# Moving four output gates and the third ranking to later steps, and replacing the last accumulating scatter, in an mLSTM and mixture-of-depths kernel

## The chip, the cores and the metric

The kernel runs on one core of a Trainium2 chip. The metric is device time in microseconds (us) of one execution, the median of several. A profile records one execution: every instruction of the five engines with its start and its duration, and the DMA transfers. The engines are TensorE (PE in the profile; its weight loads are PEld), VectorE (DVE), ScalarE (ACT), GpSimd (POOL) and SyncE (SP). Each works through its own instructions in program order and waits on semaphores for the others. Here SP issues nearly all plain DMAs, and POOL issues the indirect ones (rows by a list of indices).

## What is computed

An mLSTM cell runs over 768 time steps for 4 batches of 8 heads of 40 channels. Its output is seen as x of shape (4, 768, 320). A mixture-of-depths layer then picks the 128 best of the 768 rows of each batch and adds a gated two-layer network to these rows only:

```python
# per step t: m_new = max(f + m, i); f_stab = exp(f + m - m_new); i_stab = exp(i - m_new)
C = f_stab * C + i_stab * outer(v, k)
n = f_stab * n + i_stab * k
y = sigmoid(o_gate) * (C @ q) / max(abs(n . q), 1)
...
scores = x @ w_gate                       # (4, 768)
top = the 128 largest scores of a batch
ye = relu(x[top] @ w1) @ w2               # 320 -> 1024 -> 320
out = x.copy()
out[top] = x[top] + sigmoid(scores[top])[:, None] * ye
```

All data are 32-bit floats.

## The kernel before

The 768 time steps of a batch are cut into three chunks of 256, so that the loop over n (line 590) has 12 steps; step n works on batch b = n // 3. Steps 0 to 2 are batch 0, steps 9 to 11 batch 3. The order of all instructions is written out by hand (`manual_schedule`): what a Python call emits first comes first on its engine.

A step has these parts, in this order:

- `load(n + 3)` (line 78) has SP issue the loads of step n + 3: v (two DMAs), k (two), q (one), and gate loads `load_o` (line 70; four DMAs for one step). Three buffers hold k, q and v, four hold the gates. The dictionaries in `load` also place some stores between the loads, and they decide which gates go with which load: in the kernel before, the gates of steps 6, 7 and 8 follow q of step 9, the gate of step 9 follows q of step 10, and those of steps 10 and 11 come when `load(12)` is called, in step 9.
- `scores(n)` and `masked(n)`: the products of k and q on PE, and the causal mask on DVE (line 313).
- `turn(n + 1, "kT")` (line 232): PE transposes k of the next step, ACT copies the result out of PSUM. Its `count` is a number of filler products (`fill`, line 227) on PE ahead of the transposes, given by a tuple for steps 0 to 7. `widen` (line 223) copies q on ACT, and `turn(n + 1, "qT")` does for q what the other does for k.
- `update` and `states` (lines 266 and 278): the products of k and the weighted v on PE, and the running states on DVE. `weigh(n)` (line 248) makes the weighted v, two POOL instructions.
- `read(n)` and `attend(n)` (lines 317 and 334): the two parts of the numerator, on PE; `divide(n)` (line 343): the division on DVE, which gives y.
- `sigmoid(n)` (line 256, ACT) turns the gate into its sigmoid, `output(n)` (line 356, POOL, two instructions) multiplies it with y and writes x, `store(n)` (line 364, SP, two DMAs) writes x to the output, and `router(n)` (line 371, DVE, two products with `wg`) makes the scores of the step's 256 rows.

Once the scores of a batch are complete, the rows are ranked. `spread` (line 399) has PE write the 768 scores of the batch to all partitions and ACT copy them (`sb`). `ranks` (line 421) counts, for every row, how many scores are greater: three of the six groups of 128 rows on DVE (`greater`, line 414), three on ACT (`signs`, line 419). `select` makes a 0/1 matrix of rows and ranks, `numbers` gets the row numbers from it with small products on PE and four DVE instructions (`index`, line 457), and `fetch` (line 501) is an indirect DMA on POOL that gathers the 128 picked rows from the output in HBM into `xe`. `fetched` transposes them, `layer1` and `layer2` are the network on PE, `valued` makes the gate g of the picked rows. `weighed` (line 561) scales the result by g on ACT, and `add` (line 566) is an indirect DMA on POOL that adds it onto the rows in HBM.

The first batch's network runs in step 8, the second's in steps 9 and 10, the third's in step 11 and after the loop. The fourth batch is handled after the loop without a gather: `picked` multiplies x with the 0/1 matrix on PE. The third batch's scores are spread at the end of step 9 and ranked in step 10, beside `layer2(1)`. Where gates 6 and 7 are concerned, their sigmoids and outputs stand at the end of step 8, those of step 8 in the middle of step 9.

Two sizes that matter here: `ps_t` has two PSUM buffers shared by the transposes, by `layer2`'s result and by `fetched`; `ps_s`, `ps_u` and `ps_h` have one each.

Of the kernel before, what the change touches and what calls it, by code (L numbers as in the profile page):

```python
# [9 lines left out]
FP = mybir.dt.float32  # L10
# [3 lines left out]
OP = mybir.AluOpType  # L14
# [12 lines left out]
def _fast(ctx, tc, q, k, v, i_gate, f_gate, o_gate, w_gate, w1_in, w2_in, out):  # L27
# [6 lines left out]
    NS = S // 256  # L34
# [43 lines left out]
    def load(n):  # L78

        if n < N:  # L80
            load_kv(n, v_t, v)
            load_kv(n, k_t, k)
            for i in {8: (2,), 9: (3, 4, 5)}.get(n, ()):
                store(i)
            load_q(n)
            for i in {7: (0, 1)}.get(n, ()):
                store(i)
        for i in {7: (), 8: (), 9: (6, 7, 8), 11: (), 12: (10, 11)}.get(n, (n - 1,) if n <= N else ()):
            load_o(i)

    for t, src in ((f_sb, f_gate), (i_sb, i_gate)):
# [164 lines left out]
    def sigmoid(n):  # L256
        ACT.activation(out=o_t[n % NO], in_=o_t[n % NO], func=AF.Sigmoid)  # L257
# [98 lines left out]
    def output(n):  # L356
        b, s = divmod(n, NS)
        for r in range(2):
            x, o = x_t[b % 2][:, 2 * s + r, 0:DM], o_t[n % NO][:, r].rearrange("s h d -> s (h d)")
            order = "s (p j d) -> s j p d"  # L360
            POOL.tensor_tensor(out=x.rearrange(order, j=2, d=D), in0=pending[n]["y"][:, r].rearrange("s (j p) d -> s j p d", j=2),  # L361
                               in1=o.rearrange(order, j=2, d=D), op=OP.mult)

    def store(n):
        b, s = divmod(n, NS)
        for c in range(2):
            a = 256 * s + 128 * c
            SP.dma_start(out=out[b, a:a + 128, :].rearrange("(r t) d -> t r d", t=64),  # L368
                          in_=x_t[b % 2][64 * c:64 * c + 64, 2 * s:2 * s + 2, 0:DM])

    def router(n):
        b, s = divmod(n, NS)
        x = x_t[b % 2][:, 2 * s:2 * s + 2]
        scr = work.tile([128, DM], FP, name="scr", bufs=1)
        for r in range(2):
            DVE.tensor_tensor_reduce(out=scr, in0=x[:, r, 0:DM], in1=wg, scale=1.0, scalar=0.0,  # L376
                                     op0=OP.mult, op1=OP.add, accum_out=x[:, r, DM:DM + 1])
        del pending[n]
# [17 lines left out]

    dep = {}

    def spread(b, r0, r1):

        x, w = x_t[b % 2], r1 - r0
        pB = ps_s.tile([128, 2, 512], FP, name="pB", tag="s")
        for r in range(w):
            PE.transpose(pB[:, r // 4, 128 * (r % 4):128 * (r % 4) + 128],
                         x[:, r0 + r, DM:DM + 1].to_broadcast([128, 128]), ident)
        flat = pB.rearrange("p j t -> p (j t)")[:, 0:128 * w]
        sb = mod.tile([128, 128 * w], FP, name=f"sb{w}", bufs=1)
        ACT.copy(out=sb, in_=flat)
        return sb
# [11 lines left out]
    def ranks(b):  # L421
        x, d = x_t[b % 2], dep[b]
        d["cnt"] = mod.tile([128, 2 * NS], FP, name="cnt")
        for r in range(2 * NS):
            (greater if r < NS else signs)(b, d["sb"], x[:, r, DM:DM + 1], d["cnt"][:, r:r + 1])
        DVE.tensor_scalar(out=d["cnt"][:, NS:], in0=d["cnt"][:, NS:], scalar1=-0.5, scalar2=0.5 * (S - 1),
                          op0=OP.mult, op1=OP.add)

    def ranks_first(b):

# [120 lines left out]
    def layer2(b, f0=0, f1=NF):  # L551
        d = dep[b]
        if f0 == 0:
            if b < B - 1:
                d["py"] = ps_t.tile([128, DM], FP, name="py", tag="t")
            else:
                d["py"] = ps_h.tile([128, 2, 512], FP, name="py", tag="h")[:, 0, 0:DM]
        for f in range(f0, f1):
            PE.matmul(d["py"], d["hT"][:, f, :], w2[:, f, :], start=(f == 0), stop=(f == NF - 1))  # L559

    def weighed(b):
        d = dep[b]
        d["yg"] = mod.tile([128, DM], FP, name="yg")
        ACT.activation(out=d["yg"], in_=d["py"], func=AF.Copy, scale=d["g"])  # L564

    def add(b):
        d = dep.pop(b)
        POOL.indirect_dma_start(out=out[0:b + 1].rearrange("b s d -> (b s) d"),  # L568
                                out_offset=bass.IndirectOffsetOnAxis(ap=d["idx"], axis=0),
                                in_=d["yg"], in_offset=None, bounds_check=(b + 1) * S - 1, oob_is_err=False,  # L570
                                compute_op=OP.add)

    causal()
    other(POOL, wv_t[0])
# [15 lines left out]
    for n in range(N):  # L590
        b, s = divmod(n, NS)
        more = n + 1 < N
        late = b > 1 and s == 1
        given = late or n == 5
        if n > 0:
            load(n + 3)
        if n == 5:
            for h in range(2):
                f, g = slice(512 * h, 512 * h + 512), slice(2 * h, 2 * h + 2)
                SP.dma_start(out=w1[:, :, f], in_=w1_in[0:256, f].rearrange("(j p) f -> p j f", j=2))  # L600
                for i in range(2):
                    SP.dma_start(out=w1c[64 * i:64 * i + 64, g],
                                 in_=w1_in[256:DM, :].rearrange("p (f i e) -> p i f e", i=2, e=128)[:, i, g])
            for h in range(2):
                SP.dma_start(out=w2[:, 4 * h:4 * h + 4], in_=w2_in[512 * h:512 * h + 512].rearrange("(f p) d -> p f d", p=128))
        for i in {10: (9,), 11: (10,)}.get(n, ()):
            store(i)
        scores(n)
        masked(n)
        if n == 8:  # L610
            fetched(0)
            numbers(1, ps_t.tile([128, 3], FP, name="pi", tag="t"))
            fetch(1)
        if n == 8:
            valued(0)
        if n == 0:
            update(0)
            load(3)
            states(0)
        if n == 8:  # L620
            layer1(0, 0)
            layer1(0, 4)
            layer2(0, 0, 4)
            layer2(0, 4)
        if n == 10:
            layer2(1)
        if given:
            ranks(b - 1)
            select(b - 1)
        if n in (8, 10):  # L630
            weighed(n // 2 - 4)
        if n == 9:
            fetched(1)
            sigmoid(8)
            output(8)
            for i in range(6, 9):
                store(i)
            weigh(10)
            layer1(1, 0)
            layer1(1, 4)  # L640
            valued(1)
            router(6)
            router(7)
        early = n in (3, 6) or n > 8
        if n > 0 and early:
            router(n - 1)
        if more:
            turn(n + 1, "kT", (0, 2, 2, 2, 2, 3, 4, 5)[n] if n < 8 else 0)
            widen(n + 1)
        if 0 < n and more:  # L650
            update(n + 1)
            states(n + 1)
        if 0 < n < 7 and not early:
            router(n - 1)
        if not more:
            sigmoid(n)
            gated(n)
            fill(ps_t.tile([128, 128], FP, name="pf", tag="t"), 2)
        read(n)
        if n == 10:  # L660
            numbers(b - 1, spare(n + 1)[:, 1, 0:3])
        if n + 2 < N and n != 8:
            weigh(n + 2)
        if n == 10:
            fetch(2)
        if n == 0:
            update(1)
            states(1)
        if more:
            turn(n + 1, "qT")  # L670
            if b > 0 and s == 0:
                dep[b - 1] = {"sb": spread(b - 1, 0, 2 * NS)}
            if n not in (6, 7, 8):
                sigmoid(n)
        else:
            fetched(b - 1, 2)
            dep[b] = {"sb4": spread(b, 0, 4)}
            layer1(b - 1, 0)
            valued(b - 1)
            ranks_first(b)  # L680
        attend(n)
        divide(n)
        if n == 5:
            numbers(b - 1, spare(n + 1)[:, 1, 0:3])
        if n == 8:
            for i in (6, 7):
                sigmoid(i)
                output(i)
        elif more and n not in (6, 7):
            output(n)  # L690
        if n == 6:
            fetch(0)
        if n in (8, 10):
            add(n // 2 - 4)
        if n == 0:
            tables()
        if n == 1:
            margins()
# [9 lines left out]
    add(b - 1)  # L708
    layer1(b, 0)
    picked_numbers(b)  # L710
    layer1(b, 4)
    good = gate.tile([1, 1], I32, name="good")
    pg = ps_t.tile([1, 1 + B], FP, name="pg", tag="t")
# [360 lines left out]
```

## Time and profile before

| what | us |
|---|---|
| median of 3 runs (lowest, highest) | 168.69 (168.43, 169.73) |
| the profiled execution | 168.43 |
| its span in the profile | 166.7 |
| PE busy in it | 148.6 |
| DVE, ACT, POOL busy | 93.8, 76.2, 68.5 |
| start of the last scatter (line 568) | 160.07 |

How to read the profile: a line of the timeline gives start and length in us, the engine, the line of the kernel, the operation, the tile written and the tiles read, the shape, and how many instructions were merged; in brackets stands how long the engine had been idle before it and what ended this. A line of the waits gives engine, line and tile that waited, what for, and then total us, number of times and the longest. "SPq" and "POOLq" are the queues that issue DMAs. The rows of digits cut the span into 40 slices of 4.2 us; a digit is the busy share of a slice in tenths, and in the row PEclk the share of full clock that TensorE was granted.

### The profile page before, as it was taken

What the parts mean: (1) busy time and instruction counts of PE and PEld (TensorE: products, weight loads), DVE (VectorE), ACT (ScalarE), POOL (GpSimd) and SP (SyncE); (2) the same over time, 40 slices, a digit from 0 to 9 for tenths busy, and PEclk for the clock granted to TensorE, in tenths of its full rate; (3) what the DMA queues carried; (4) which work ended last, traced back from release to release, by engine and by line L of the source; (5) the groups of instructions that cost most, each with busy time, mean ns of one, the idle gap of its engine ahead of it and who ended that gap; (6) DMA issues with size and microseconds to landing.
All of it is one profiled execution on the core that took longest, in us unless ns stands there. A gap on an engine that the chain in (4) does not pass through costs nothing.

```text
span 166.7 us, 6707 instructions
## 1 busy us (share of the span) xinstructions
PE 148.6 (89%) x2872; PEld 128.1 (77%) x2872; DVE 93.8 (56%) x250; ACT 76.2 (46%) x144; POOL 68.5 (41%) x89
## 2 busy tenths in 40 slices
PE   7889999699999599999999997959999999999910
PEld 7679888497989489999888696839778888799700
DVE  6477455566764967859950038743894787701000
ACT  1577474154545744478231354255845149521110
POOL 7046292928281733753006017871800673130030
PEclk9999999999999959999999999999999999999997
DMA  4999988899987978999989997799788360330012
GB/s 85 196 160 160 169 142 142 152 154 179 152 142 129 169 125 137 271 172 274 366 211 182 230 163 121 125 199 176 132 160 219 93 118 4 81 39 0 8 18 37
DMA packets 94424, 24.14 MB, mean 145 GB/s; under 512 B 88465, under 2 KB 93778, under 8 KB 94386
## 3 DMA queue, kind: packets, MB, share of 16 engines
q1 hardware_dynamic: 93472, 22.36, 71.0%
q0 software_dynamic: 720, 1.15, 4.1%
q8 instruction: 24, 0.39, 0.9%
q10 hardware_dynamic: 194, 0.13, 0.3%
q14 instruction: 14, 0.11, 0.2%
HBM read 19.04 MB, written 4.59 MB: 142 GB/s over the span
## 4 chain that ended last, share of the span: by engine, by line
PE 56%; DMA 19%; issue 7%; SPq 5%; POOL 4%; DVE 2%; ACT 2%; ACTq 1%; POOLq 1%; DVEq 0%
PE pt L241 10%; DMA k<-in_k_dram 9%; PE pU L274 9%; PE pH L329 6%; PE pH L339 5%; PE py L559 5%; PE pS L307 5%; PE pU L543 5%; DMA o<-in_o_gate_dram 4%; DMA out_dram<-yg,idx 3%; SPq L368 3%; DMA i_sb<-in_i_gate_dram 2%; POOL x L361 2%; PE pt L230 2%; PE pX L479 2%
## 5 line engine op out<-in xcount | busy, mean ns | idle before, releaser
L253 POOL TENSOR_TENSOR wv<-v,cols 64x656 f32<-64x656 f32 x23 | 30.5, 1328 | 50.3 <-DMA v<-in_v_dram 36.1
L361 POOL TENSOR_TENSOR x<-y,o 128x320 f32<-128x320 f32 x24 | 20.7, 881 | 9.5 <-ACT o L257 4.8
L245 ACT COPY qT<-pt 128x512 f32<-128x512 f32 x24 | 13.8, 634 | 20.3 <-PE pt L241 20.3
L243 ACT COPY kT<-pt 128x512 f32<-128x512 f32 x24 | 13.6, 586 | 19.6 <-PE pt L241 19.5
L241 PE MATMUL pt<-ident,k 128*128 128x128 f32 x96 | 14.9, 286 | 6.3 <-DMA k<-in_k_dram 5.8
L286 DVE TENSOR_TENSOR C<-pU,C 128x164 f32<-128x164 f32 x40 | 13.1, 328 | 9.6 <-PE pU L274 8.5
L274 PE MATMUL pU<-wv,k 128*64 128x82 f32 x384 | 17.6, 246 | 0.7 <-POOL wv L253 0.5
L559 PE MATMUL py<-w,hT 128*128 128x320 f32 x64 | 18.2, 437 | 0.0
L241 PEld LDWEIGHTS pt<-ident,k 128*128 128x128 f32 x96 | 10.8, 144 | 9.6 <-DMA k<-in_k_dram 4.1
L274 PEld LDWEIGHTS pU<-wv,k 128*64 128x64 f32 x384 | 15.5, 144 | 2.8 <-issue 1.2
L339 PE MATMUL pH<-wv,P 128*64 128x82 f32 x384 | 16.7, 237 | 0.1
L376 DVE CUSTOM_DVE_ANT_0 scr<-x,wg 128x320 f32<-128x320 f32 x22 | 14.1, 642 | 4.0 <-POOL x L361 2.1
L339 PEld LDWEIGHTS pH<-wv,P 128*64 128x64 f32 x384 | 14.5, 136 | 2.2 <-issue 1.8
L559 PEld LDWEIGHTS py<-w,hT 128*128 128x128 f32 x64 | 11.8, 190 | 4.7
L313 DVE TENSOR_TENSOR P<-pS,mask 128x1024 f32<-128x1024 f32 x12 | 14.6, 1216 | 1.5 <-PE pS L307 1.4
L307 PE MATMUL pS<-qT,kT 40*64 40x64 f32 x768 | 14.2, 221 | 0.5 <-ACT qT L245 0.3
L329 PE MATMUL pH<-C,qT 40*64 40x41 f32 x704 | 14.4, 229 | 0.1
L329 PEld LDWEIGHTS pH<-C,qT 40*64 40x64 f32 x704 | 12.8, 134 | 1.7 <-issue 0.7
L307 PEld LDWEIGHTS pS<-qT,kT 40*64 40x64 f32 x768 | 12.5, 134 | 1.8 <-ACT qT L245 0.5
L568 POOL DMA_INDIRECT out_dram<-yg,idx x4 | 6.4, 1605 | 16.9 <-ACT yg L564 16.3
L241 PE MATMUL pt<-ident,qw 128*128 128x128 f32 x96 | 13.1, 279 | 0.0
L419 ACT ACTIVATE sgn<-sb,x 128x768 f32<-128x768 f32 (+2 forms) x16 | 12.8, 800 | 0.4
(138 smaller groups left out, 212.1 us busy)
## 6 DMA issues: line engine op xcount, KB each, us to landing
k<-in_k_dram SPq DMA_DIRECT2D x24, 160.0 KB, 5.0
q<-in_q_dram SPq DMA_DIRECT2D x12, 320.0 KB, 5.5
v<-in_v_dram SPq DMA_DIRECT2D x24, 160.0 KB, 4.7
o<-in_o_gate_dram SPq DMA_DIRECT2D x48, 80.0 KB, 4.2
out_dram<-x SPq DMA_DIRECT2D x24, 160.0 KB, 2.9
w<-in_moe_w_dram SPq DMA_DIRECT2D x2, 640.0 KB
w<-in_moe_w_dram SPq DMA_DIRECT2D x2, 512.0 KB
w1c<-in_moe_w_dram SPq DMA_DIRECT2D x4, 64.0 KB, 6.2
```

Of the source, the lines that this page charges most:

```text
L241: PE.transpose(pt[:, p, :], src[:, c, 2 * p:2 * p + 2, :].rearrange("s j d -> s (j d)"), ident)
L243: ACT.copy(out=T[:, :, 128 * c:128 * c + 128], in_=pt)
L245: ACT.copy(out=T.rearrange("e p (u t) -> e t p u", t=2)[:, c], in_=pt)
L253: (DVE if n == 0 and r else POOL).tensor_tensor(out=wv_t[n % 3][o, :, :, r], in0=v_t[n % NB][o], op=OP.mult, in1=cols[s][o, 0:2, b * H:b * ...
L274: PE.matmul(pU[64 * j:64 * j + 64, c, p], k_t[n % NB][:, c, 2 * p + j, :], wv_t[n % 3][:, c, 2 * p + j], start=True, stop=True)
L307: PE.matmul(pS[o, j, c, p, :], kT[e, p, t], qT[e, p, t], start=True, stop=True)
L313: DVE.tensor_tensor(out=P.rearrange(flat), in0=pending[n].pop("pS").rearrange(flat), op=OP.mult, in1=mask.unsqueeze(1).to_broadcast([128, ...
L329: PE.matmul(g["pH"][64 * c:64 * c + 64, NP * j + p, r], g["qT"][e, p, t], state[n, 2 * c + r][e, p, :], start=(c, j) not in g["begun"], st ...
L339: PE.matmul(g["pH"][64 * c:64 * c + 64, NP * j + p], g["P"][:, j, c, p, :], wv_t[n % 3][:, c, 2 * p + j], start=(c, j) not in g["begun"], ...
L361: POOL.tensor_tensor(out=x.rearrange(order, j=2, d=D), in0=pending[n]["y"][:, r].rearrange("s (j p) d -> s j p d", j=2), in1=o.rearrange(o ...
L376: DVE.tensor_tensor_reduce(out=scr, in0=x[:, r, 0:DM], in1=wg, scale=1.0, scalar=0.0, op0=OP.mult, op1=OP.add, accum_out=x[:, r, DM:DM + 1])
L559: PE.matmul(d["py"], d["hT"][:, f, :], w2[:, f, :], start=(f == 0), stop=(f == NF - 1))
```

## The change

Seven things change.

1. The gates of steps 6, 7 and 8 are loaded behind q of step 10 instead of q of step 9, the gate of step 9 behind q of step 11 instead of q of step 10, and the gates of steps 10 and 11 at the end of step 9, behind the stores of steps 6 to 8, instead of at its beginning.
2. The sigmoids and outputs of steps 6, 7 and 8 move into the second half of step 9: gate 6 behind `widen(10)`, gates 7 and 8 behind the transposes of q of step 10. Routers 6, 7 and 8 follow in step 9; routers 7 and 8 stand behind `divide(9)`. The sigmoid and output of step 9 move to step 10, behind the transposes of q of step 11, router 9 to step 11, and store 9 to step 11.
3. The third batch's `spread` moves from the end of step 9 into step 10, between twelve and four of the sixteen products of `layer2(1)`, in a PSUM buffer of `ps_h`. Its six counts are cut in two: three on DVE and one on ACT ahead of the last four products, two on ACT behind `weighed(1)`.
4. `weigh(11)` moves from step 9 to the beginning of step 10.
5. The fillers ahead of the transposes of k in step 5 go from 3 to 8.
6. For the last batch, `fetch(3)` gathers the picked rows into `xe` after their numbers are known, and `weighed` computes `py * g + xe` in one DVE instruction instead of `py * g` on ACT.
7. The last scatter writes these rows without adding.

The diff, with the lines that carry this:

```diff
-        for i in {7: (), 8: (), 9: (6, 7, 8), 11: (), 12: (10, 11)}.get(n, (n - 1,) if n <= N else ()):
+        for i in {7: (), 8: (), 9: (), 10: (6, 7, 8), 11: (9,), 12: ()}.get(n, (n - 1,) if n <= N else ()):
             load_o(i)
...
-    def spread(b, r0, r1):
+    def spread(b, r0, r1, pool=None):
...
+            pB = pool.tile([128, 2, 512], FP, name="pB", tag="h")
...
+    def halved(d):
         DVE.tensor_scalar(out=d["cnt"][:, NS:], in0=d["cnt"][:, NS:], scalar1=-0.5, scalar2=0.5 * (S - 1),
                           op0=OP.mult, op1=OP.add)
+
+    def ranks_third(b, begin):
+        x, d = x_t[b % 2], dep[b]
+        if begin:
+            d["cnt"] = mod.tile([128, 2 * NS], FP, name="cnt")
+            for r in range(NS):
+                greater(b, d["sb"], x[:, r, DM:DM + 1], d["cnt"][:, r:r + 1])
+        for r in (NS,) if begin else range(NS + 1, 2 * NS):
+            signs(b, d["sb"], x[:, r, DM:DM + 1], d["cnt"][:, r:r + 1])
+        if not begin:
+            halved(d)
...
     def weighed(b):
...
+        if b == B - 1:
+            DVE.scalar_tensor_tensor(out=d["yg"], in0=d["py"], scalar=d["g"], in1=xe_t[b % 2][:, 0:DM], op0=OP.mult, op1=OP.add)
+            return
...
-                                compute_op=OP.add)
+                                **({} if b == B - 1 else {"compute_op": OP.add}))
...
-        for i in {10: (9,), 11: (10,)}.get(n, ()):
+        for i in {11: (9, 10)}.get(n, ()):
             store(i)
...
         if n == 10:
-            layer2(1)
-        if given:
+            weigh(11)
+            layer2(1, 0, 6)
+            dep[2] = {"sb": spread(2, 0, 2 * NS, ps_h)}
+            ranks_third(2, True)
+            layer2(1, 6)
+        elif given:
             ranks(b - 1)
             select(b - 1)
         if n in (8, 10):
             weighed(n // 2 - 4)
+        if n == 10:
+            ranks_third(2, False)
+            select(2)
         if n == 9:
             fetched(1)
-            sigmoid(8)
-            output(8)
-            for i in range(6, 9):
-                store(i)
             weigh(10)
             layer1(1, 0)
             layer1(1, 4)
             valued(1)
-            router(6)
-            router(7)
-        early = n in (3, 6) or n > 8
+        early = n in (3, 6) or n > 10
+        if n == 11:
+            router(9)
...
-            turn(n + 1, "kT", (0, 2, 2, 2, 2, 3, 4, 5)[n] if n < 8 else 0)
+            turn(n + 1, "kT", (0, 2, 2, 2, 2, 8, 4, 5)[n] if n < 8 else 0)
             widen(n + 1)
+            if n == 9:
+                sigmoid(6)
+                output(6)
...
-        if n + 2 < N and n != 8:
+        if n + 2 < N and n not in (8, 9):
             weigh(n + 2)
...
             turn(n + 1, "qT")
-            if b > 0 and s == 0:
+            if n in (3, 6):
                 dep[b - 1] = {"sb": spread(b - 1, 0, 2 * NS)}
-            if n not in (6, 7, 8):
+            if n == 9:
+                for i in (7, 8):
+                    sigmoid(i)
+                    output(i)
+                router(6)
+            elif n == 10:
+                sigmoid(9)
+                output(9)
+                sigmoid(10)
+            elif n not in (6, 7, 8):
                 sigmoid(n)
...
         divide(n)
...
-        if n == 8:
-            for i in (6, 7):
-                sigmoid(i)
-                output(i)
-        elif more and n not in (6, 7):
+        if n == 9:
+            router(7)
+            router(8)
+            for i in range(6, 9):
+                store(i)
+            load_o(10)
+            load_o(11)
+        elif more and n not in (6, 7, 8):
             output(n)
...
     picked_numbers(b)
+    fetch(b)
     layer1(b, 4)
```

More of the change, by code (lines that the diff above doesn't have):

```diff
@@ L397, in _fast @@
     dep = {}
-    def spread(b, r0, r1):
+    def spread(b, r0, r1, pool=None):
         x, w = x_t[b % 2], r1 - r0
-        pB = ps_s.tile([128, 2, 512], FP, name="pB", tag="s")
+        if pool is None:
+            pB = ps_s.tile([128, 2, 512], FP, name="pB", tag="s")
+        else:
+            pB = pool.tile([128, 2, 512], FP, name="pB", tag="h")
         for r in range(w):
@@ L425, in ranks @@
             (greater if r < NS else signs)(b, d["sb"], x[:, r, DM:DM + 1], d["cnt"][:, r:r + 1])
+        halved(d)
+    def halved(d):
         DVE.tensor_scalar(out=d["cnt"][:, NS:], in0=d["cnt"][:, NS:], scalar1=-0.5, scalar2=0.5 * (S - 1),
                           op0=OP.mult, op1=OP.add)
+    def ranks_third(b, begin):
[7 more added lines that the diff above has]
+        if not begin:
+            halved(d)
     def ranks_first(b):
```

## The prediction, made before the change was run

> **What bounds the kernel now.** I read the page's summary first, then what TensorE (PE) waited for, then the order of time around each edit. Shares and slices:
>
> ```profile
> span 166.7 us, 6707 instructions
> PE 148.6 (89%) x2872; PEld 128.1 (77%) x2872; DVE 93.8 (56%) x250; ACT 76.2 (46%) x144; POOL 68.5 (41%) x89
> PEclk9999999999999959999999999999999999999997
> DMA  4999988899987978999989997799788360330012
> ```
>
> PE is the bound; the DMA engines are nearly full until 125 us (slice 30), so loads arrive in the order that SP issues them. What PE itself waited for between 75 and 146 us:
>
> ```profile
> PE pU L543 <- ACT xeT L516: 1.5, 2, 1.2
> PE pt L241 <- DMA k<-in_k_dram: 1.5, 1, 1.5
> PE pU L274 <- POOL wv L253: 0.5, 1, 0.5
> PE pt L241 <- ACT yg L564: 0.4, 2, 0.2
> ```
>
> So some 3.2 us of waits lie in step 9 (1.17 + 1.50 + 0.54). Their causes, in order of time (start, length, instruction, idle before):
>
> ```profile
> 102.07 0.74 ACT L257 ACTIVATE o<-o 128x640 f32<-128x640 f32 x1 [1.61 <-DMA o<-in_o_gate_dram]
> 103.12 2.05 PE L543 MATMUL pU<-xeT,w 128*128 128x128 f32 x16 [1.17 <-ACT xeT L516]
> 107.85 1.14 DVE L376 CUSTOM_DVE_ANT_0 scr<-x,wg 128x320 f32<-128x320 f32 x1 [0.74 <-POOL x L361]
> 108.59 1.53 POOL L253 TENSOR_TENSOR wv<-v,cols 64x656 f32<-64x656 f32 x1
> 109.14 1.34 DVE L376 CUSTOM_DVE_ANT_0 scr<-x,wg 128x320 f32<-128x320 f32 x1
> 110.62 0.63 PE L241 MATMUL pt<-ident,k 128*128 128x128 f32 x4 [1.50 <-DMA k<-in_k_dram]
> 111.79 1.35 PE L274 MATMUL pU<-wv,k 128*64 128x82 f32 x32 [0.54 <-POOL wv L253]
> ```
>
> The sigmoid of step 7 held ACT, which owed PE xeT; k of step 10 was issued behind the gate loads 6 to 8. The DVE lines matter later: a router product (L376) takes 0.49 alone, but beside POOL it ends only 0.36 after POOL's current instruction (109.14 to 110.48, POOL to 110.12).
>
> The wait in step 5, and the last instructions:
>
> ```profile
> 55.20 0.94 PE L230 MATMUL pt<-hot 128*128 128x128 f32 x6
> 58.04 1.78 PE L241 MATMUL pt<-ident,k 128*128 128x128 f32 x8 [1.91 <-DMA k<-in_k_dram]
> 59.76 2.45 PE L274 MATMUL pU<-wv,k 128*64 128x82 f32 x32
> ```
> ```profile
> 159.27 0.53 ACT L564 ACTIVATE yg<-py,g 128x320 f32<-128x320 f32 x1 [4.07 <-PE py L559]
> 160.07 1.56 POOL L568 DMA_INDIRECT out_dram<-yg,idx  x1 [12.30 <-ACT yg L564]
> ```
>
> After 58.04 PE ran at half clock (granted 0.57 in 58.2 to 61.6). The kernel ends on the accumulating scatter: issued 160.07, landed 4.5 later, 2.1 of closing.
>
> **Base.** The profiled run took 168.43 (span 166.7 plus 1.7 around it); the median of the runs is 168.69, so 0.26 above. Changes are summed on 168.43.
>
> **Fills of step 5** (3 to 8). Ten more matmuls, about 1.4 (step 7's ten took 1.38), inside the 1.91 wait: no cost; without that cover, 1.4. If they keep the clock, L241 and L274 fall from 1.78 and 2.45 to their usual 1.04 and 1.35: 1.8 at step 6. But step 8's transposes of the gathered rows begin at 83.35, and the gather (issued 76.94, landing 6.3) came at 83.24; it waits for a store in SP's full queue, which PE does not hurry. Bounds 0 and -0.1; I take -0.1. The skill's "TensorE: Matmul & The Clock Gate", section "Why this matters for your kernels", allows PE gaps up to about 3 us, so by it the fills would change nothing: 0. The trace differs: 1.91 idle, 1.49 busy of 3.4, and then the half clock.
>
> **Loads.** After q9 (92.70) SP now issues v10, k10, q10, the twelve gates 6 to 8, v11, k11, q11, then gate 9. With the rows' own issue times (1.54, 2.55, 0.75, 8.91, 1.20, 1.78, 1.01, 3.95): k10 is issued by 97.5 instead of 106.4 and lands near 102.5 (median 5.0), gate 8 near 111.3, k11 near 116, gate 9 is issued by 115.3. Stores 6 to 8 follow their outputs, then the eight DMAs of gates 10 and 11 (6.96 before). SP's queue is in order: store 8 waits for output 8 (118.0, below) and holds the eight behind it; they land near 128, their sigmoids come at 129. Cover 1 us, priced 1 for 1 beyond it. Stores 9 and 10 move to step 11; only the last gather, 23 us on, needs them: 0.
>
> **Step 9 on PE.** ACT no longer owes two sigmoids: layer 1 starts at 102.4 (step 8's same pair had a 0.4 gap) instead of 103.12, and its 5.3 ends 107.7. k10 is there, and wv10 too (POOL has only the add ahead of it, 102 to 105). Transposes to 109.0, update 110.4, read 111.5, queries 112.55, attend 113.9 (pB, 0.66, has left), scores of step 10 end 115.05, before 118.26. A lead of 3.2. The add of batch 0 also leaves POOL 3 us earlier (no output 6 and 7 ahead of it); nobody waits for it.
>
> **Where the lead goes.** Sigmoid 6 fits where ACT idled 2.04 before the queries; 7 and 8 follow at 113.3 and 114.0. POOL: output 6 111.3 to 113.0, outputs 7 and 8 from 114.05. DVE: divide to 115.6, then routers 7 and 8, with masked(10) queued behind them. By the collision above, router products end at 116.1, 117.2, 118.3, and the last, which meets the first half of weigh(11), at 119.9; without collisions 118.1. PE has the twelve layer-2 matmuls to 118.5 (12 x 0.286) and then waits in the third batch's spread. I count from S, its effective start: 119.4 with collisions (five of six transposes go early), 118.5 without.
>
> From S, ACT is in series: pB 0.86, sb copy 0.83, sign 1.05, yg 0.46, two signs 2.18, two kT copies 0.98, widen 0.73: S+7.1. Before, the signs lay under layer 2; now kT and widen of step 11 stand behind them. Queries to S+8.15, attend S+9.45, scores of step 11 S+10.6 = 130.0, before 130.09. The lead is gone. Counting and select (DVE, S+6.5) stay under ACT; weigh(11), now at the head of step 10 on POOL, ends at 121.1, 2 us before update(11) reads it.
>
> **Step 11.** The fills, the read, fills and xe transposes (4.1 in all before) bring PE to the spread at S+14.15, layer 1 at S+14.9 if it waits for nothing: 134.3, before 134.19. But output 9 is now behind fetch(2) (idx S+8.2, 0.9 to its start, 1.05: S+10.15), output 10 behind that, and router 9 and 10 come together: with collisions they end S+15.6, layer 1 at 135.25. So the middle is +0.1 to +1.1 by this S. I take +0.6, since DVE does get in between POOL's instructions at times (104.24, 0.92). Add(1) and the gated products slip by about 1 on POOL, with 2 in hand before router_last. After that PE is the chain to the end; a shift passes on whole.
>
> **Tail.** fetch(3): idx at 152.9, 0.9, POOL 1.05, landing 3.0 after start (fetch(2)): 156.8, 2.4 before py ends; the add before it landed at 150.3, the stores near 146. Hidden; beyond 2.4 late it costs in full. POOL is free for the register load at 155.1. The sum's new wait, for that gather, has only the scatter behind it. The VectorE sum replaces ACT's 0.53; between 0.33 (L286, 164 columns) and 0.82 (L353, 640) it is 0.5: 0. The plain scatter is not in the trace. Not longer than the accumulating one (4.5; 0 gain), not shorter than a plain store's 2.6 (gain 1.9). Nearest is the gather of the same rows, 3.0, of which POOL 1.05; with a store's receipt I take 3.3: -1.2. The skill's "DMA: Bandwidth & Descriptors", section "Anatomy of one DMA — SWDGE (gpsimd) path", gives 2.0 us plus bytes over 436 GB/s, an estimate of 2.4 here, so -2.1 and 166.8 in all; the gather's 3.0 is above its figure.
>
> **Sum.** 168.43 - 0.1 + 0.6 - 1.2 = 167.7.
>
> **Rivals.**
> Faster: no collisions. S = 118.5, layer 1 at 133.4 (-0.8), scatter 3.1 (-1.4): 166.2. For it: POOL's spans are rough, and L376 took 0.49 beside an indirect DMA at 105.32. Against: 69.05, 107.85 and 109.14 collided.
> Scatter no quicker: its landing is all receipt. 168.43 - 0.1 + 0.6 = 168.9. For it: 2.9 of the 4.5 come after POOL; against: the gather.
> Slower: the last router of step 8 waits for both halves of weigh(11), ending 121.4 (POOL 121.05 + 0.36), S = 120.9, layer 1 at 136.75, +2.6: 168.43 - 0.1 + 2.6 - 1.2 = 169.7; and PE would have idled 2.3 in one piece, which in step 5 (1.91) brought the half clock, up to 1.7 more: 171.4. It decides once layer 1 starts past 135.5. For it: the pile on POOL; against: DVE has gone between two POOL instructions each time seen.
>
> **Chances.** Forecast 0.45 (own range 166.9 to 168.6), faster rival 0.25, scatter rival 0.15, slower rival 0.15. About 1% (1.7 us, against 168.69: 167.0 and 170.4) is what a measurement of this kernel can tell from no change. Faster by more: most of the faster rival and a little of the forecast, 0.30; slower by more: over half of the slower rival, 0.09; within, 0.61. The range leaves out a fifth: 165.9 (the rival at its cheap scatter) to 169.6.
>
> **What would show it.** Right: no k or xeT wait in step 9; pB of batch 2 waiting on L376 near 119 to 120; kT copies of step 11 behind the signs; scores of step 11 ending near 130; a PE gap before L404 in step 11; the last scatter landing 3.3 after issue; clock full near 60 us but layer 1 of step 8 still near 84.3. Wrong: xe of step 8 landing earlier (then the fills are worth up to 1.8), gates 10 or 11 holding ACT, PE waiting for xe at the last sum, or the spread of batch 2 never waiting.

## The result, and the profile after

The changed kernel is slower. Its median is 173.5 us (172.91 to 176.01, four runs) against 168.56 of the kernel before (166.97 to 169.73, four runs); the ratio is 1.031, 95% interval 1.021 to 1.042. Executions of one and the same kernel on one chip lie up to 6% apart here, so the ratios, here and below, compare only the runs within 1.5% of the fastest of their kernel, and where too few of these were left, no ratio is given. Ratios are always against the kernel before on the same chip; its median was between 167.4 and 171.8 from chip to chip.

The profiled execution took 173.79, its span is 172.0. Line numbers are shifted a little in the changed kernel: the spread is now L407, the transposes of picked rows L532, layer 1 L561, layer 2 L577, `weighed` L584 and L586, the scatter L590. The page's summary:

```profile
span 172.0 us, 6732 instructions
PE 152.5 (89%) x2882; PEld 132.8 (77%) x2882; DVE 95.5 (55%) x251; ACT 75.1 (44%) x143; POOL 69.7 (40%) x90
PEclk9999999999999999579999999999999987999998
```

PE is busy for the same 89%, but there are two dips in its clock, near 70 and near 140 us; before there was one, near 59. What PE waited for between 75 and 150 us (waits, as before: total, times, longest):

```profile
PE pB L407 <- DVE x L376: 4.1, 4, 2.6
PE pU L516 <- DVE C L286: 1.1, 1, 1.1
PE pt L241 <- ACT yg L586: 1.1, 2, 0.9
PE pU L561 <- ACT xeT L534: 0.8, 2, 0.5
```

The waits of step 9 for k, xeT and the weighted v (3.2 us) have gone down to 0.5. In their place stands 4.1 us of waiting for VectorE's routers (L376), of which one piece is 2.6.

To see where the difference arises, I cut the time at five points that every kernel of this study has, each read from PE's timeline: A, layer 1 of the first batch starts (step 8); B, scores of step 10 end; C, scores of step 11 end; D, layer 1 of the third batch starts (step 11); E, the last result of layer 2 ends.

| | A | A to B | B to C | C to D | D to E | E to the end | span |
|---|---|---|---|---|---|---|---|
| before | 84.33 | 33.9 | 11.8 | 4.0 | 25.1 | 7.5 | 166.7 |
| after | 86.72 | 30.4 | 15.25 | 6.9 | 26.55 | 6.2 | 172.05 |
| difference | +2.4 | -3.5 | +3.4 | +2.9 | +1.5 | -1.4 | +5.3 |

The lines behind these numbers, from the timeline of the changed kernel. Steps 5 and 6:

```profile
55.05 2.05 PE L230 MATMUL pt<-hot 128*128 128x128 f32 x16
67.63 0.63 PE L241 MATMUL pt<-ident,k 128*128 128x128 f32 x4 [1.88 <-DMA k<-in_k_dram]
```

The sixteen filler products cover the wait of step 5 as meant. The next step's k is now what PE waits for (1.88), and the half clock follows there, for 6.83 us (before it was 3.41, behind the wait of step 5).

Step 9:

```profile
105.07 2.05 PE L561 MATMUL pU<-xeT,w 128*128 128x128 f32 x16 [0.46 <-ACT xeT L534]
110.32 1.09 PE L241 MATMUL pt<-ident,k 128*128 128x128 f32 x8
```

Layer 1 waits 0.46 for xeT instead of 1.17, and all eight transposes of k run in one piece. The spread of the third batch in step 10:

```profile
120.04 3.02 POOL L253 TENSOR_TENSOR wv<-v,cols 64x656 f32<-64x656 f32 x2
120.57 1.34 DVE L376 CUSTOM_DVE_ANT_0 scr<-x,wg 128x320 f32<-128x320 f32 x1
121.98 0.32 PE L407 MATMUL pB<-ident,x 128*128 128x128 f32 x1 [0.84 <-DVE x L376]
126.50 1.05 ACT L243 COPY kT<-pt 128x512 f32<-128x512 f32 x2
```

The last router of step 8 stands beside the first half of weigh(11) and takes 1.34 instead of 0.49; PE waits for it, and the copies of k on ACT come late after the signs. Step 11:

```profile
131.62 3.60 POOL L361 TENSOR_TENSOR x<-y,o 128x320 f32<-128x320 f32 x4
135.38 1.67 POOL L590 DMA_INDIRECT out_dram<-yg,idx  x1 [0.16 <-issue]
136.36 2.74 DVE L376 CUSTOM_DVE_ANT_0 scr<-x,wg 128x320 f32<-128x320 f32 x1
136.52 2.22 POOL L385 TENSOR_TENSOR ow<-o,wg 128x320 f32<-128x320 f32 x2
139.17 0.32 PE L407 MATMUL pB<-ident,x 128*128 128x128 f32 x1 [2.57 <-DVE x L376]
139.33 2.77 PE L561 MATMUL pU<-xeT,w 128*128 128x128 f32 x16
```

Outputs 9 and 10 (L361) follow the gather, the scatter of batch 1 follows them, and then the two gated products `ow` (L385) begin 0.16 after the last product of router 10 has begun. That product takes 2.74 us and PE, which needs its scores, waits 2.57. What this does to the clock is seen in PE's busy time and granted clock (PEclk, behind POOL's share) of two neighbouring stretches:

```profile
136.00:139.40 3.40, 0.56 (x3) 0.37 (x4) 3.22 (x5) 0.00 (x1) 2.75 (x3) 1.00 0.85 154
139.40:142.80 3.40, 3.40 (x23) 3.17 (x24) 0.24 (x2) 0.59 (x1) 0.00 (x0) 0.63 0.00 0
```

PE is busy for 0.56 of 3.40 us, and in the next 3.40 its clock is 0.63: layer 1 takes 2.77 instead of 2.05. The tail, answering to the last two instructions shown of before:

```profile
165.92 0.55 DVE L584 SCALAR_TENSOR_TENSOR yg<-py,g,xe 128x320 f32<-128x320 f32 x1 [4.18 <-PE py L577]
166.75 1.03 POOL L590 DMA_INDIRECT out_dram<-yg,idx  x1 [5.27 <-DVE yg L584]
```

The plain scatter needs 1.03 on POOL and lands 2.8 after its issue, against 1.56 and 4.5; 2.5 us of closing follow, against 2.1.

### The profile page after: what moved, and what is told of

It is laid out like the page before. It is cut to its first block, busy times and chain, and to the rows that moved or that the text cites. A ratio compares the mean times of both kernels' runs of the same rounds, so it can differ in the third digit from the quotient of the medians.

```text
span 172.0 us, 6732 instructions
## 1 busy us (share of the span) xinstructions
PE 152.5 (89%) x2882; PEld 132.8 (77%) x2882; DVE 95.5 (55%) x251; ACT 75.1 (44%) x143; POOL 69.7 (40%) x90
## 4 chain that ended last, share of the span: by engine, by line
PE 65%; DMA 10%; DVE 9%; issue 6%; ACT 4%; POOL 2%; DVEq 0%; SPq 0%; POOLq 0%; ACTq 0%
PE pt L241 11%; PE pU L274 9%; DMA k<-in_k_dram 9%; PE pH L329 6%; PE pH L339 6%; PE pU L561 6%; PE py L577 5%; PE pS L307 5%; DVE scr L376 4%; PE warm L107 3%; PE ph L561 2%; PE pt L230 2%; PE pU L565 2%; DMA xe<-out_dram,idx 2%; PE pB L407 2%
## 5 line engine op out<-in xcount | busy, mean ns | idle before, releaser
L361 POOL TENSOR_TENSOR x<-y,o 128x320 f32<-128x320 f32 x24 | 21.2, 909 | 17.5 <-DVE x L394 8.3
L376 DVE CUSTOM_DVE_ANT_0 scr<-x,wg 128x320 f32<-128x320 f32 x22 | 17.3, 786 | 3.7 <-POOL x L361 1.9
L577 PE MATMUL py<-w,hT 128*128 128x320 f32 x64 | 18.4, 437 | 0.0
L241 PE MATMUL pt<-ident,k 128*128 128x128 f32 x96 | 14.3, 282 | 3.9 <-DMA k<-in_k_dram 2.8
L577 PEld LDWEIGHTS py<-w,hT 128*128 128x128 f32 x64 | 11.8, 191 | 4.5
L241 PE MATMUL pt<-ident,qw 128*128 128x128 f32 x96 | 13.9, 291 | 0.0
L417 DVE TENSOR_SCALAR_CACHE_REDUCE cmp<-sb,x 128x768 f32<-128x768 f32 (+2 forms) x14 | 12.0, 857 | 0.4
```

The costliest lines, as they stand in the source:

```text
L241: PE.transpose(pt[:, p, :], src[:, c, 2 * p:2 * p + 2, :].rearrange("s j d -> s (j d)"), ident)
```

## The experiments

The theory after the result: the 2.9 us in step 11 come from the last router product of step 10 standing beside POOL's `ow` products, and the half clock behind it from PE idling 2.57 in one piece. Rivals: the fillers of step 5 set the whole later course; the late outputs alone delay the routers; the gates have nothing to do with it and the tail is the cost. The measured numbers in one table (ratio to before on the same chip, with its 95% interval; stages as above):

| kernel | ratio | A to B | B to C | C to D | D to E |
|---|---|---|---|---|---|
| fills 3 | 1.014 [1.006, 1.021] | 30.9 | 15.6 | 7.3 | 26.6 |
| ow on VectorE | 0.986 [0.977, 0.996] | 32.9 | 15.6 | 5.05 | 25.0 |
| both | 0.989 [0.983, 0.996] | 31.4 | 15.6 | 5.05 | 25.0 |
| before, new tail | 0.983 [0.975, 0.991] | 39.5 | 11.8 | 3.6 | 25.0 |
| 12 fillers in step 11 | 1.030 [1.021, 1.038] | 32.9 | 15.25 | 6.9 | 25.0 |
| half of ow on VectorE | none | 32.6 | 15.3 | 6.2 | 26.4 |
| both, weigh(11) in step 9 | 1.035 [1.025, 1.046] | 30.0 | 21.6 | 4.9 | 25.0 |
| lighter gate order | none | 37.0 | 11.8 | 3.55 | 25.0 |
| the same, weigh(10) first | none | 33.6 | 11.8 | 6.7 | 26.75 |
| before, new tail, weigh(10) first | 0.987 [0.979, 0.995] | 33.0 | 11.9 | 4.4 | 25.1 |
| lighter order, store 8 first | 0.975 [0.956, 0.995] | 34.9 | 12.0 | 3.7 | 25.0 |

A to B lies mostly between 30 and 34. The three long ones (39.5, 37.0, 34.9) have 10.2, 6.8 and 3.4 us of half clock in step 9; but "ow on VectorE", "12 fillers" and "half of ow" (32.6 to 32.9) have 3.4 us there too. Each row of stages is one profiled execution.

**The fillers of step 5 put back** (changed kernel, one number).

```diff
-            turn(n + 1, "kT", (0, 2, 2, 2, 2, 8, 4, 5)[n] if n < 8 else 0)
+            turn(n + 1, "kT", (0, 2, 2, 2, 2, 3, 4, 5)[n] if n < 8 else 0)
```

> The changed kernel with 3 fillers in step 5 again instead of 8; all else as changed. Theory (the fillers cost time): with eight, PE comes to step 6 1.9 us early, idles 1.88 us for k there and runs 6.8 us at half clock, so that layer 1 of step 8 starts at 86.7 instead of 84.3. Undone, it starts near 84.3 and the time falls by 2.4, from 173.5 to about 171. Rival (the fillers are neutral, as the prediction had it: the gathered rows of step 8 set the pace, and the half clock is chance of its windows): 173 to 174, and layer 1 of step 8 no earlier.

The steps from C on stay as in the changed kernel (7.3 and 26.6), so the fillers aren't what makes step 11 slow. The ratio rests on two runs of four (174.06 and 173.55; the profiled one took 177.74) and does not settle what the fillers themselves cost. A, the start of layer 1 in step 8, was 86.7, 86.6, 83.5 and 85.2 in the four kernels with eight fillers and 82.7 to 89.7, mean 85.4, in the nine with three. The +2.4 in the table above is within that scatter.

**The gated products on VectorE**, behind `valued` in its order, so that POOL has no product beside router 10 (the scatter of batch 1 still is there) and VectorE itself can't collide.

```diff
-            POOL.tensor_tensor(out=ow[:, r].rearrange("s (j p d) -> s j p d", j=2, d=D),
+            DVE.tensor_tensor(out=ow[:, r].rearrange("s (j p d) -> s j p d", j=2, d=D),
...
-            gated(n)
...
             valued(b - 1)
+            gated(n)
```

> The changed kernel with the two products of the last gate and wg (ow, 2.2 us on POOL beside router 10) made by VectorE instead, behind the router products and the g of the third batch; 8 fillers kept. Theory (VectorE stands behind POOL): the last product of router 10 takes 0.5 instead of 2.74, PE's 2.57 us wait in the spread of step 11 shrinks to under 0.5, and without that idle piece the half clock after it (about 1.3 us) goes too: 173.5 - 2.2 - 1.3 = about 170. Rival (outputs 9 and 10 are late anyway, behind the third batch's ranks): at most 0.5 is gained, 173 or more.

```profile
139.36 0.49 DVE L376 CUSTOM_DVE_ANT_0 scr<-x,wg 128x320 f32<-128x320 f32 x1
139.91 0.32 PE L407 MATMUL pB<-ident,x 128*128 128x128 f32 x1 [0.32 <-DVE x L376]
```

The last router product is back at 0.49 and PE waits 0.32 for it: C to D falls from 6.9 to 5.05, and D to E from 26.55 to 25.0, since the half clock is gone with the long idle. These 3.4 us are the effect that the theory named. The ratio falls further than that (1.031 to 0.986), but these two were taken on different chips. The comparison on one chip is between the two kernels with three fillers, "fills 3" and "both" (next), which differ in this edit alone: 1.014 [1.006, 1.021] against 0.989 [0.983, 0.996], about 4.2 us, of which C to D (7.3 to 5.05) and D to E (26.6 to 25.0) account for 3.9. That is the cause of the loss in step 11 shown in time, not only in the profile.

**Both** edits together.

> Both: 3 fillers in step 5, and the products with wg on VectorE. Theory: the two losses are separate places and add up: 173.5 - 2.4 - 3.5 = 167.6, near the kernel before less its tail gain. Rival (one of the two only hides behind the other, or both are chance of the clock): 170 or more.

0.989 against 0.986, with C to D and D to E the same to 0.01: on this chip the fillers make no difference that can be told. The 2.4 that the expectation had added for the fillers does not show. No stretch of half clock is in this profile.

**Only the tail** of the change, on the kernel before (fetch(3), the sum on VectorE, the plain scatter).

> The kernel before with the tail of the change alone: the last rows gathered, summed on VectorE, scattered without adding. Theory: the tail's gain of 1.3 to 1.4, read from yg to the end of the span (7.4 before, 6.1 after), stands by itself: 168.6 - 1.4 = 167.2. Rival (the tail is shorter only because the changed kernel's last stage runs on an emptier chip, or the gather of the rows delays the POOL queue): no gain, 168.6.

0.983, with E to the end at 6.0 instead of 7.5. By the stage, 1.5 us, the tail is worth what the prediction said and a little more (the ratio, 1.7%, rests on two runs of four), and the rest of the change more than takes it back. Even with `ow` out of the way ("both"), no gain of the rest over the tail alone shows (0.989 and 0.983, with overlapping intervals): what step 9 saves (A to B) is paid in B to C, and 1.05 to 1.5 more in C to D, where routers 9 and 10 follow two late outputs.

**Fillers against the half clock**: twelve instead of two ahead of the transposes of the picked rows in step 11, which shortens PE's idle time without touching the wait.

```diff
-            fetched(b - 1, 2)
+            fetched(b - 1, 12)
```

> The changed kernel with 12 filler products instead of 2 on PE ahead of the transposes of the third batch's rows in step 11 (2.7 us of work, laid into the 3.2 us that PE waits in the spread there); products with wg still on POOL beside router 10. It tells the wait from the half clock that follows it. Theory (both count): the half clock after the spread goes (layer 1 back to 2.05 from 2.77, w1c products to 0.71 from 1.23), the wait of router 10 stays 2.7: 1.3 faster than the changed kernel, which by ratio stands at 1.031 of the kernel before, so about 1.023. Rival (the wait alone counts and the clock falls or not by chance): no change, 1.031.

```profile
138.37 0.32 PE L407 MATMUL pB<-ident,x 128*128 128x128 f32 x1 [1.44 <-DVE x L376]
138.53 1.95 PE L561 MATMUL pU<-xeT,w 128*128 128x128 f32 x16
```

The idle time is 1.44 instead of 2.57, layer 1 runs at full clock (1.95) and D to E is 25.0; C to D stays at 6.9, because the router ends no earlier. In these profiles this separates the two costs: 1.5 us of the loss is the clock, 1.85 the collision. The mean granted clock points the same way in every run: 0.984 to 0.988 in the four of this kernel, 0.958 to 0.974 in the four of the changed one. But the ratio (1.030) does not show the gain of 1.3 us that was expected, and by it alone the rival (no change) stands. The profiled execution took 2.5 us longer from A to B than that of the changed kernel, with a stretch of half clock of its own in step 9; whether the other runs did so too was not seen.

**One of the two products on VectorE**: `gated(n, 0)` issues the first on POOL as before, `gated(n, 1)` the second on VectorE, behind `valued`.

```diff
-            gated(n)
+            gated(n, 0)
...
             valued(b - 1)
+            gated(n, 1)
```

> The changed kernel with one of the two products with wg on POOL, the other on VectorE behind router 10: half the dose. Theory (a two-input VectorE product ends 0.36 us after the POOL instruction beside it): the last product of router 10 takes 1.3 to 1.7 instead of 2.74; PE's wait falls by 1.1 to 1.4, and the idle piece, now under 1.5 us, no longer costs the clock: ratio near 1.010, between the whole (1.031) and none (0.986 to 0.989). Rival (the second POOL instruction does not matter, the product waits for the add's DMA on POOL): 2.7 as before, 1.03.

```profile
137.01 1.93 DVE L376 CUSTOM_DVE_ANT_0 scr<-x,wg 128x320 f32<-128x320 f32 x1
137.18 1.41 POOL L387 TENSOR_TENSOR ow<-o,wg 128x320 f32<-128x320 f32 x1
```

With one product instead of two the router takes 1.93, between 0.49 and 2.74, and ends 0.35 after POOL, as in the other cases (136.36 + 2.74 - 138.74 = 0.36). The length follows POOL's. Two points of the expectation missed: PE's wait fell only to 1.76, and a wait of that length was still followed by half clock (D to E 26.4). In time the experiment is inconclusive: the runs lie between 167.07 and 174.35.

**weigh(11) earlier**, in step 9 ahead of output 6, to free router 8 (on "both").

```diff
-            weigh(11)
             layer2(1, 0, 6)
...
             if n == 9:
+                weigh(11)
                 sigmoid(6)
                 output(6)
```

> As e3 (3 fillers, products with wg on VectorE), and the two POOL instructions of weigh(11) moved ahead of output 6 in step 9, so that they no longer stand beside the last product of router 8. Theory (the third batch's ranks wait for VectorE behind POOL): that product takes 0.5 instead of 1.34, the spread of step 10 starts about 0.8 earlier unless output 6 is pushed back by as much (v of step 11 lands near 112.5, the two take 2.6): 0.3 to 0.8 faster than e3's ratio 0.989. Rival (POOL's whole queue is full there, the 2.6 us just move): outputs 7 and 8 end 1 us later, 0 to 1 slower than e3.

```profile
115.03 2.63 POOL L253 TENSOR_TENSOR wv<-v,cols 64x656 f32<-64x656 f32 x2 [7.46 <-DMA v<-in_v_dram]
122.42 0.87 PE L407 MATMUL pB<-ident,x 128*128 128x128 f32 x3 [4.48 <-DVE y L353]
```

Slower (1.035), and my theory of it fell: POOL stood 7.46 us in front of a v that had not been loaded, outputs 6 to 8 stood behind it, and router 6 behind output 6 kept VectorE from dividing. PE waited 4.48 in one piece. An in-order queue passes a wait on to everything behind it; the place of weigh(11) in the change is the better one.

**A lighter order of the gates**: the kernel before with the new tail, gates 6 and 7 as they were, and only gate 8 (and the load of gate 9) behind q of step 10; the third batch is ranked as before.

```diff
-        for i in {7: (), 8: (), 9: (6, 7, 8), 11: (), 12: (10, 11)}.get(...)
+        for i in {7: (), 8: (), 9: (6, 7), 10: (8, 9), 11: (), 12: (10, 11)}.get(...)
...
             widen(n + 1)
+            if n == 9:
+                sigmoid(8)
+                output(8)
+                store(8)
...
             turn(n + 1, "qT")
+            if n == 9:
+                router(8)
```

> The kernel before with the tail of the change, and of the rest only this: gate 8 is loaded behind q of step 10 (gates 6 and 7 stay ahead), its sigmoid and output stand behind the widening of step 10, router 8 behind the states; ranks stay beside layer 2. Theory (k of step 10 was late by four gate DMAs or more, and the ranks are best left under layer 2): PE's 1.5 us wait for k in step 9 and the 0.5 for wv go, router 8 costs 0 to 0.5 in the spread: 1 to 2 us faster than the tail alone, ratio 0.975 to 0.985. Rival (the lead is lost again in the spread of step 9, behind output 8): the tail alone, 0.983 to 0.992.

```profile
108.86 1.28 POOL L253 TENSOR_TENSOR wv<-v,cols 64x656 f32<-64x656 f32 x1 [2.19 <-DMA out_dram<-yg,idx]
110.20 1.50 PE L274 MATMUL pU<-wv,k 128*64 128x82 f32 x32 [2.05 <-POOL wv L253]
```

B to C is 11.8 and C to D 3.55: nothing of the loss behind step 9 remains. This kernel leaves the ranking where it was, but also weigh(11) and gates 6 and 7, so which of them it is that costs B to C its 3.4 us is not singled out by a run. But the wait for k in step 9 only gave way to one of 2.05 for the weighted v, whose second half stood on POOL behind the landing of batch 0's scatter; 6.8 us of half clock followed. The runs spread from 164.85 to 169.92, so there is no ratio.

**The same with weigh(10) ahead of that scatter.**

```diff
+        if n == 8:
+            weigh(10)
         if n in (8, 10):
             add(n // 2 - 4)
...
-            weigh(10)
             layer1(1, 0)
```

> The third experiment kind: is there a version that beats both kernels? It takes over from the change the tail, and of the gates only that those of step 8 and 9 are loaded behind q of step 10; the sigmoid, the output and the store of step 8 stand behind the widening of q of step 10, router 8 behind the transposes of its q, and the third batch is ranked as in the kernel before. New is that weigh(10) stands on POOL ahead of the scatter of batch 0, not behind it. Theory (the second product of weigh(10) stood behind the scatter's landing: 2.19 us on POOL, 2.05 on PE in the kernel without the move, and the half clock followed): the wait of PE at L274 in step 9 falls below 0.5, layer 1 of step 8 to the scores of step 10 takes 31 to 32 us instead of 37.0, scores of step 10 to those of step 11 stay at 11.8, from there to layer 1 of batch 2 at 3.6, and the ratio to before is 0.96 to 0.98. Rival (the product waited for something else, its v for instance, or the next thing is late by as much): PE's wait stays at about 2 or moves to the transposes of k, and the ratio is 0.98 to 0.99, as with the tail alone.

```profile
133.74 1.06 POOL L504 DMA_INDIRECT xe<-out_dram,idx  x1 [9.76 <-DVE P L313]
136.71 0.90 PE L514 MATMUL pX<-ident,xe 128*128 128x128 f32 x3 [2.72 <-DMA xe<-out_dram,idx]
```

PE's wait for the weighted v in step 9 is gone, so the theory of that wait holds. The rival's other half holds too: something else is late by as much. The store of step 8 stood in SP's queue behind eight gate loads (it was issued from 125.4), the gather needs it, and PE waited 2.72 for its rows in step 11, with half clock from the middle of this wait on (D to E 26.75). Runs from 167.84 to 172.92, no ratio.

**Tail and weigh(10) alone**, all gates as before.

> The kernel before with the change's tail and with weigh(10) ahead of the scatter of batch 0 on POOL; all gates as before. Theory: the wait of PE for the weighted v in step 9 (0.54 in before, 2.13 in the profile of the tail alone) goes, those for xeT and k (1.2 and 1.5 in before) stay, and the ratio is 0.975 to 0.985, a little under the tail alone (0.983). Rival (only the gates' order matters): no difference to the tail alone, 0.983 and PE idle in step 9 as before.

0.987 [0.979, 0.995], not to be told from the tail alone, as the rival had it. In the profile the wait for the weighted v is gone, those for xeT (1.06) and k (1.56) are there.

**The lighter order with the gates of steps 10 and 11 behind store 8.**

```diff
-        for i in {..., 11: (), 12: (10, 11)}.get(...)
+        for i in {..., 11: (), 12: ()}.get(...)
...
                 store(8)
+                load_o(10)
+                load_o(11)
```

> The kernel with the tail, the lighter gate order and weigh(10) ahead of the scatter, with one more move: the gates of steps 10 and 11 are loaded behind the store of step 8, not ahead of it. Theory (in the kernel without this move the store of step 8 stood in SP's queue behind these eight loads, so that the gather of batch 2 started at 133.74 and TensorE waited 2.72 us for its rows, with half clock after it): that wait falls below 0.5, scores of step 11 to layer 1 of batch 2 takes 3.5 to 4 us instead of 6.7, layer 1 to the last result of the network 25.0, the span is 164 to 166 and the ratio to before 0.965 to 0.985. Rival (one thing late makes room for the next: output 8 now stands behind the scatter's landing on POOL, and the gates of 10 and 11 behind it): the sigmoid of step 10 comes late, routers 9 and 10 with it, layer 1 of batch 2 is again 1 to 3 us late, and the ratio is 0.985 to 1.0.

PE no longer waits for the gathered rows, C to D is 3.7 and D to E 25.0. What is left in the middle is a wait of 1.48 for xeT in step 9. The ratio is 0.975 [0.956, 0.995], from two runs of six and three of eleven; the medians of all runs are 167.69 against 170.96. This version beats both kernels. That it also beats the tail alone (0.983) is within the intervals and not shown.

## Why the prediction was wrong

Forecast 167.7, measured 173.5. Step by step:

- **Fills of step 5: -0.1 was taken.** The wait in step 5 is gone as foreseen, the next k is waited for instead, and layer 1 of step 8 moved by +2.4 in the profiled execution. Over all kernels the start scatters from 82.7 to 89.7 with no difference between three and eight fillers that can be told. The reason I gave, that the gather sets the pace and not PE, did not hold in this execution: the rows had landed at 82.9, and PE came to their transposes at 85.72, behind the 1.88 us for k and the 6.83 us of half clock of step 6. It did hold in "half of ow", also with eight fillers, where PE waited 1.27 for the rows. How much of the +2.4 belongs to the fillers stays open.
- **Lead of step 9: 3.2.** Measured 3.5. Right, by the waits named.
- **The lead is lost at the spread and on ACT: scores of step 11 at 130.0.** Shifted by the +2.4 of A that is 132.4; they ended at 132.41. Router 8 was to end at 119.9 with collisions, or 122.3 shifted; it ended at 121.91. Right in the end, with lead and loss each 0.3 larger than forecast; for this place the collision as read from the trace was good.
- **Step 11: layer 1 at most 1.1 later, +0.6 taken.** This is the step that failed. It came 2.9 later. I counted routers 9 and 10 beside outputs 9 and 10, and stopped there. Of the next thing on POOL I wrote only that "the gated products slip by about 1 on POOL, with 2 in hand before router_last": I looked at who waits for `ow`, and not at who stands beside it. With the outputs late, router 10's last product came to lie beside `ow`. The price was in the profile of before, where the same `ow` had a product of `valued` beside it that nobody waited for:

```profile
133.85 3.10 DVE L524 CUSTOM_DVE_ANT_0 scr<-xe,wg 128x320 f32<-128x320 f32 x1
134.35 2.23 POOL L385 TENSOR_TENSOR ow<-o,wg 128x320 f32<-128x320 f32 x2
```

  3.10 us instead of 0.49, hidden in before only because router 10 had ended at 133.8. This row also speaks against two of my readings, that a product ends 0.36 after POOL's current instruction, and that VectorE "has gone between two POOL instructions each time seen": here it waited out both `ow` products. Moving the products to VectorE took 1.85 of the 2.9 away; the 1.05 left has the size of the part that I had priced (0.1 to 1.1), but was not tried by itself.
- **"After that PE is the chain to the end; a shift passes on whole."** It passed on with 1.5 more. PE had idled 2.57 in one piece and then ran at half clock; with twelve fillers there and the same wait, D to E was 25.0 again. The slower rival had this term (1.7), tied to another wait. The Trainium skill's "TensorE: Matmul & The Clock Gate", section "Why this matters for your kernels", would allow gaps up to about 3 us; 2.57, and 1.88 in step 6, were followed by half clock here, so the measurement decides against it (which pieces were followed by it and which were not is listed in the last section).
- **Tail: -1.2.** Measured -1.4 from E to the end (7.5 to 6.2). The scatter landed in 2.8, not 3.3, and the closing was 0.4 longer. The Trainium skill's "DMA: Bandwidth & Descriptors", section "Anatomy of one DMA — SWDGE (gpsimd) path", gave an estimate of 2.4, nearer than mine.

**The rivals.** "Slower" had the right form: routers late behind a pile on POOL, PE idle for more than 1.9 us in one piece, half clock. It put the pile a step too early (at router 8 and weigh(11), which cost only what the forecast said) and gave it 0.15. Its own point of decision, layer 1 past 135.5, was passed: 139.33, or 136.9 without the +2.4. "Scatter no quicker" and "no collisions" are refuted by the 2.8 and by the 1.34 and 2.74.

The sum with the measured terms: 166.7 + 2.4 - 3.5 + 3.4 + 2.9 + 1.5 - 1.4 = 172.0, the span of the profile. Without the scattering +2.4 it would be 169.6. What the change gains in step 9 it gives back by the spread that ACT has to pass through in step 10, as forecast; the loss is the collision in step 11 and the clock after it, and the +2.4 ahead of step 8, whose cause is open.

## What to carry to other kernels

When instructions move, list for each engine pair that disturbs each other which instruction will lie beside which afterwards, and look up the price of every such pair in the trace of before, also where it is hidden there because nobody waits. A wait of PE of over two microseconds in one piece is to be priced with the half clock behind it (here each of more than 2.1 us had it), and fillers ahead of it can buy that part back. In an order of in-order queues a wait that is taken away shows the next one (k, then the weighted v, then a store, here); each step of such a chain is found by a run and not by adding up.

## What the runs showed of the hardware

- A VectorE product of two SBUF tiles (128x320) takes 0.49 us alone or beside an indirect DMA on POOL, 1.34 beside a weighting product, 1.93 beside one `ow` product and 2.74 beside two, and ends 0.35 us after POOL each time. Between two weighting products it gets in (1.34: POOL's first ends at 121.56, the product at 121.91, POOL's second at 123.06); the two `ow` products, of which the second begins 0.6 before the first ends, it waits out both.
- Half clock, in the 13 profiles from 20 us on: it came during or just behind each of the six idle pieces of PE of more than 2.1 us (2.13 to 4.48). From 1.4 to 2.1 us it went either way: it came with pieces of 1.48, 1.68, 1.76, 1.83, 1.88, 1.91 and 2.05, and not with those of 1.50 (the kernel before, step 9), 1.70 and 1.75 ("both") and 1.99 and 2.06 ("before, new tail, weigh(10) first"). Three stretches came with no piece over 1.1 us near them (step 9 of "ow on VectorE", "12 fillers" and "half of ow"). A stretch lasts about 3.4 us, one to three come in a row, and they fall on different steps in different kernels. They are a part of why runs of one kernel differ, but not all of it: of the kernel before on one chip, a run of 167.59 had a mean clock of 0.985 and one of 170.97 had 0.994.
- An indirect scatter that writes takes 1.03 us on POOL and lands 2.8 to 3.0 after its issue; the one that accumulates takes 1.6 and lands after 4.0 to 5.6. Of weigh(10), issued behind the accumulating one on POOL, the second half started only when that had landed (after 2.35 us of idle time in the changed kernel, 2.19 in the lighter order); an output in the same place went ahead at once (the kernel with the tail and weigh(10) first: scatter at 110.75 for 1.62, output at 112.44). The trace shows why: that second half waits for the semaphore of the scatter, and the output does not. So this is a wait in the program, not one of the engine; with weigh(10) first it stands ahead of weigh(11), at 116.83, when the scatter has landed (115.66).
